# Two decode-attention blocks on one core: the last projection in two PSUM banks with two copiers, and both output stores on SyncE's queue

## Chip, cores, metric

One Trainium2 chip, one core of it. The metric is the device time of one execution in microseconds (us). The kernel before takes 2563.64 us (median of six runs, 2563.62 to 2563.99).

## The reference

Two independent blocks, A and B, each a single-token decode step: 8 batch rows, 32 heads of width 128, a cache of 4096 keys and values per head, all in bf16. Their outputs are concatenated.

```python
def block(x, k_cache, v_cache, wq, wo):            # once for A, once for B
    q = (x @ wq).reshape(B, 1, H, 128).transpose(0, 2, 1, 3)
    scores = einsum("bhqd,bhkd->bhqk", q, k_cache) * 128 ** -0.5
    o = einsum("bhqk,bhkd->bhqd", softmax(scores), v_cache)
    return o.transpose(0, 2, 1, 3).reshape(B, 1, H * 128) @ wo     # wo: 4096 x 1024
```

## The kernel before

The kernel streams all caches once through a ring of three 8 MB SBUF slots. Each engine is given a list of operations, and a dependency becomes a semaphore wait only where it is needed. Only the end matters here. Block B's output weights `wo` arrive in four pieces of 20, 8, 3 and 1 of 32 rows, so that little is left to multiply when the last piece lands. Block A is c = 0, block B is c = 1 = NC - 1.

```python
NT, DT = 4, 256                       # 4 column tiles of 256 output columns
wo_cuts = ((0, 20), (20, H - 4), (H - 4, H - 1), (H - 1, H))
proj, pv_ps = ps("proj"), ps("pv")    # two PSUM banks; pv_ps is free after the last attention tile
...
def make_proj(c):
    w = tile_of("wo", c)
    for i, (r0, r1) in enumerate(wo_cuts if c == NC - 1 else ((0, H),)):
        def emit(e, r0=r0, r1=r1):
            for r in range(r0, r1):
                for q in range(NT):
                    col = r * D + q * DT
                    x = e.matmul(proj[32 * q:32 * (q + 1), 0:DT], on_sb[:, c, r:r + H * B:HQ],
                                 w[:, col:col + DT], start=(r == 0), stop=(r == H - 1), tile_position=(0, 32 * q))
            return x
        opProj[c] = add("pe", emit, [opNorm[c], opT[("wo", c, i)], c_pad, opEv.get(c - 1)])
    opEv[c] = add("dve", lambda e: e.tensor_copy(orow[:, c, :], proj[:, 0:DT]), [opProj[c]])
    outs.append(dma(out[...], orow[0:128:32 // B, c, :], ("out", 0),
                    [opEv[c]] if c == NC - 1 else [opEv[c], opT[("wo", NC - 1, len(wo_cuts) - 1)]],
                    "sp" if c == NC - 1 else "act"))
...
make_norm(1); make_proj(0); make_proj(1)
```

The four matmuls of a row go to four column tiles of the array and run side by side. The trace shows that one `matmul` is two PE instructions, a weight load and a matmul. The first store (A's half of the output) waits for the last weight piece, presumably so that it does not get between the loads.

## Time and profile before

| | before |
|---|---|
| time, median of 6 runs | 2563.64 us |
| span of the profiled execution | 2562.6 us |
| DMA | over 90% busy in all 40 slices, 432 GB/s |
| VectorE, the busiest engine | 85% |

The lines below are from the page of the kernel before: DMA activity by slice, the queues that carry instructions and data, and the chain of waits.

```profile
DMA  9999999999999999999999999999999999999999
...
q1 hardware_dynamic: 19476, 1107.32, 99.9%
q8 instruction: 7, 0.11, 0.0%
...
DMA 52%; DVE 28%; issue 16%; PE 4%; ACT 0%; another core or an unknown queue 0%; DVEq 0%; SPq 0%
```

The kernel is bound by its loads. The change touches only what comes after the last attention tile, so its effect can only be in the last microseconds. They are in the timeline (start in us, duration in us, engine, line, operation, what it writes and reads, how many; in brackets PE's idle time before and what ended it):

```profile
2552.50 4.24 PE L431 MATMUL proj<-ring,on_sb 128*32 128x256 bf16 x80 [5.70 <-DMA ring<-in_B_wo_dram]
2557.31 0.86 PEld L431 LDWEIGHTS proj<-ring,on_sb 128*32 128x32 bf16 x32 [0.82 <-DMA ring<-in_B_wo_dram]
2557.31 1.10 PE L431 MATMUL proj<-ring,on_sb 128*32 128x256 bf16 x32 [0.58 <-DMA ring<-in_B_wo_dram]
...
2559.17 0.96 PE L431 MATMUL proj<-ring,on_sb 128*32 128x256 bf16 x16 [0.76 <-DMA ring<-in_B_wo_dram]
...
2559.84 0.65 ACTq L208 DMA_DIRECT2D out_dram<-orow  x1
2560.19 0.42 DVE L435 CAST orow<-proj 128x256 bf16<-128x256 f32 x1 [12.91 <-PE proj L431]
2560.64 0.69 SPq L208 DMA_DIRECT2D out_dram<-orow  x1
```

Every piece's matmuls wait for a DMA: PE is always ahead of the weights. After the last weights come four matmuls, one copy of 0.42 us and the store.

### The profile page before, as it was taken

What the parts mean: (1) busy time and instruction counts of PE and PEld (TensorE: products, weight loads), DVE (VectorE), ACT (ScalarE), POOL (GpSimd) and SP (SyncE); (2) the same over time, 40 slices, a digit from 0 to 9 for tenths busy, and PEclk for the clock granted to TensorE, in tenths of its full rate; (3) what the DMA queues carried; (4) which work ended last, traced back from release to release, by engine and by line L of the source; (5) the groups of instructions that cost most, each with busy time, mean ns of one, the idle gap of its engine ahead of it and who ended that gap; (6) DMA issues with size and microseconds to landing.
All of it is one profiled execution on the core that took longest, in us unless ns stands there. A gap on an engine that the chain in (4) does not pass through costs nothing.

```text
span 2562.6 us, 18832 instructions
## 1 busy us (share of the span) xinstructions
PE 1118.0 (44%) x7712; PEld 397.3 (16%) x7712; DVE 2170.6 (85%) x1042; ACT 129.8 (5%) x401; POOL 2.6 (0%) x15
## 2 busy tenths in 40 slices
PE   2443443443444444444434444444444434434435
PEld 0111111111111111111111111111111111111112
DVE  3898898898898898898898888988988988988983
ACT  1100000000000000000000000000000000000000
POOL 0000000000000000000000000000000000000000
PEclk8767676766767766766767666766757666666657
DMA  9999999999999999999999999999999999999999
GB/s 425 427 438 430 436 432 436 432 436 432 436 432 436 430 437 430 436 432 435 432 435 431 435 433 433 435 433 435 432 436 432 435 433 435 433 435 433 435 433 394
DMA packets 19554, 1107.51 MB, mean 432 GB/s; under 512 B 2184, under 2 KB 2248, under 8 KB 2520
## 3 DMA queue, kind: packets, MB, share of 16 engines
q1 hardware_dynamic: 19476, 1107.32, 99.9%
q8 instruction: 7, 0.11, 0.0%
q10 hardware_dynamic: 68, 0.05, 0.0%
q14 instruction: 3, 0.02, 0.0%
HBM read 1107.33 MB, written 0.03 MB: 432 GB/s over the span
## 4 chain that ended last, share of the span: by engine, by line
DMA 52%; DVE 28%; issue 16%; PE 4%; ACT 0%; another core or an unknown queue 0%; DVEq 0%; SPq 0%
DMA ring<-in_A_k_cache_dram 25%; DMA ring<-in_B_k_cache_dram 25%; DVE ring L330 10%; DVE ring L335 10%; PE red L345 4%; DVE s_sb L353 4%; DVE PM L370 3%; DMA ring<-in_B_wo_dram 2%; DVE rmax L359 1%; DVE rtmp L360 0%; ACT PM L291 0%; PE o L285 0%; DVEq L135 0%; DVE ngm L363 0%
## 5 line engine op out<-in xcount | busy, mean ns | idle before, releaser
L330 DVE TENSOR_TENSOR ring<-ring,qbc 128x8192 bf16<-128x8192 bf16 x256 | 1131.8, 4421 | 309.7 <-DMA ring<-in_B_k_cache_dram 152.9
L345 PE MATMUL red<-ring,ident 128*128 128x512 bf16 x2048 | 782.6, 552 | 1391.7 <-DVE ring L335 1391.7
L335 DVE TENSOR_TENSOR ring<-ring 128x4096 bf16<-128x4096 bf16 x256 | 582.2, 2274 | 0.0
L345 PEld LDWEIGHTS red<-ring,ident 128*128 128x128 bf16 x2048 | 239.1, 127 | 1843.5 <-DVE ring L335 1494.1
L353 DVE TENSOR_REDUCE s_sb<-red 128x64 f32<-128x1024 f32 x256 | 311.9, 1218 | 3.5 <-PE red L345 3.5
L382 PE MATMUL pv<-ring,PM 128*32 128x512 bf16 x4096 | 273.3, 414 | 4.7 <-DVE PM L370 4.7
L370 DVE TENSOR_TENSOR PM<-pe,own_h 128x2048 bf16<-128x2048 bf16 x64 | 146.2, 2285 | 0.7 <-ACT pe L365 0.7
L382 PEld LDWEIGHTS pv<-ring,PM 128*32 128x32 bf16 x4096 | 103.6, 103 | 187.4 <-issue 114.3
L319 ACT ACTIVATE qbc<-misc 128x128 bf16<-128x128 f32 x64 | 17.7, 277 | 1091.7 <-PE misc L317 1091.7
L365 ACT ACTIVATE pe<-s_sb,ngm 128x256 bf16<-128x256 f32 x64 | 32.5, 508 | 466.7 <-DVE ngm L363 466.7
L390 ACT ACTIVATE accS<-pv 128x512 bf16<-128x512 f32 x64 | 38.2, 597 | 352.9 <-PE pv L382 352.9
L399 PEld LDWEIGHTS o<-accS,E 128*32 128x32 bf16 x1024 | 31.3, 100 | 49.6 <-issue 48.4
L399 PE MATMUL o<-accS,E 128*32 128x32 bf16 x1024 | 38.1, 185 | 0.7 <-ACT accS L390 0.7
L405 ACT ACTIVATE o_sb<-o 32x32 f32 (+1 forms) x64 | 11.8, 185 | 452.4 <-PE o L399 444.5
L359 DVE TENSOR_REDUCE rmax<-s_sb 128x1 f32<-128x256 f32 x64 | 26.9, 420 | 2.2
L435 DVE CAST orow<-proj 128x256 bf16<-128x256 f32 x2 | 0.8, 424 | 27.4 <-PE proj L431 27.4
L431 PE MATMUL proj<-ring,on_sb 128*32 128x256 bf16 x256 | 12.7, 377 | 15.8 <-DMA ring<-in_A_wo_dram 8.7
L305 DVE COPY qT<-misc 128x64 bf16<-128x64 bf16 x8 | 3.5, 435 | 18.6 <-PE misc L301 18.6
L312 ACT ACTIVATE qst<-qT 128x128 bf16 (+1 forms) x64 | 18.7, 293 | 1.9 <-DVE qT L305 1.9
L360 DVE TENSOR_SCALAR rtmp<-half,rmax 128x32 f32<-128x32 f32 x64 | 15.4, 241 | 2.3
L363 DVE TRANSPOSE_TENSOR_REDUCE ngm<-rtmp 128x1 f32<-128x32 f32 x64 | 13.6, 212 | 2.2
L317 PE MATMUL misc<-ident,qst 128*128 128x128 bf16 x64 | 14.7, 230 | 0.9 <-ACT qst L312 0.9
(33 smaller groups left out, 66.1 us busy)
## 6 DMA issues: line engine op xcount, KB each, us to landing
ring<-in_B_wo_dram SPq DMA_DIRECT2D x1, 5120.0 KB, 33.2
ring<-in_B_wo_dram SPq DMA_DIRECT2D x1, 2048.0 KB, 37.8
ring<-in_B_wo_dram SPq DMA_DIRECT2D x1, 768.0 KB, 39.1
ring<-in_A_k_cache_dram SPq DMA_DIRECT2D x32, 39.9
ring<-in_A_v_cache_dram SPq DMA_DIRECT2D x32, 27.8
ring<-in_B_k_cache_dram SPq DMA_DIRECT2D x32, 39.8
ring<-in_B_v_cache_dram SPq DMA_DIRECT2D x32, 27.8
ring<-in_B_wo_dram SPq DMA_DIRECT2D x1, 256.0 KB, 39.3
```

The costliest lines, as they stand in the source:

```text
L312: return e.activation(qst[:, n % 2, :].rearrange("p (j m) -> p j m", m=MP), from_.unsqueeze(2).to_broadcast([128, HQ, MP]), ACTF.Copy)
L319: opQbc[n] = add("act", lambda e: e.activation(qbc[:, n % 2, :], misc[:, 0:Dh], ACTF.Copy), [opQb[n], _at(opMul, NR * (n - 2) + NR - 1)])
L330: opMul[s] = add("dve", lambda e: e.tensor_tensor(v, v, qbc[:, n % 2, :].unsqueeze(1).to_broadcast([128, CT, Dh]), ALU.mult), [opT[("k", n ...
L335: return add("dve", lambda e: e.tensor_tensor(v[:, :, 0:64], v[:, :, 0:64], v[:, :, 64:128], ALU.add), [opMul[s]])
L345: i = e.matmul(dst, ident[:], v[:, g, :, j, :], start=(j == 0), stop=(j == 3))
L353: opRed[s] = add("dve", lambda e: e.tensor_reduce(s_sb[:, n % 2, r * CT:(r + 1) * CT], red_ps[s % 2][:, :].rearrange("p (t w) -> p t w", w ...
L359: m = add("dve", lambda e: e.tensor_reduce(rmax[:], s_sb[:, n % 2, :], AX.X, ALU.max), [opRed[NR * n + NR - 1]])
L365: opExp[n] = add("act", lambda e, at: e.activation(pe[:], s_sb[:, n % 2, :], ACTF.Exp, bias=ngm[:, n % 2:n % 2 + 1], scale=scale, accum_ou ...
L370: opPM[n] = add("dve", lambda e: e.tensor_tensor(PM[:], pe[:].unsqueeze(2).to_broadcast([128, T, HQ]), own_h[:].unsqueeze(1).to_broadcast( ...
L382: i = e.matmul(pv_ps[32 * q:32 * (q + 1), :], PM[:, t:t + 4, :].rearrange("p t j -> p (t j)"), v[:, t * Dh:(t + 4) * Dh], start=(g == 0), ...
L390: opAcc[n] = add("act", lambda e: e.activation(accS[:], pv_ps[:], ACTF.Copy), [opPV[n], _at(opExt, n - 1)])
L399: x = e.matmul(to, E[:, i, PH - 1 - u:PH - 1 - u + MB], accS[:, i * 128 + H * u:i * 128 + H * (u + 1)], start=(i == 0 and u == 0), stop=(i ...
```

## The change

Intent: the single copy of 256 columns is the only arithmetic left between the last matmul and the store. With the columns in two banks, VectorE and ScalarE can each copy half at the same time; the Trainium skill, "TensorEngine Tiling (Array Packing)", section "PSUM Bottleneck", gives the same advice, to use both engines to empty PSUM (what that was worth here is measured in e8). The first store also leaves ScalarE, whose queue is then free for its copy.

```diff
+            banks = (proj, pv_ps) if c == NC - 1 else (proj,)
+            dt = DT // len(banks)
             for i, (r0, r1) in enumerate(wo_cuts if c == NC - 1 else ((0, H),)):
-                ... 4 matmuls of DT = 256 columns a row into proj ...
+                for f, bank in enumerate(banks):
+                    def emit(e, r0=r0, r1=r1, f=f, bank=bank):
+                        for r in range(r0, r1):
+                            for q in range(NT):
+                                col = r * D + q * DT + f * dt
+                                x = e.matmul(bank[32 * q:32 * (q + 1), 0:dt], on_sb[:, c, r:r + H * B:HQ],
+                                             w[:, col:col + dt], start=(r == 0), stop=(r == H - 1), tile_position=(0, 32 * q))
+                        return x
+                    opProj[(c, f)] = add("pe", emit, [..., opAcc[NQ - 1]] + opEv.get(c - 1, []))
-            opEv[c] = add("dve", lambda e: e.tensor_copy(orow[:, c, :], proj[:, 0:DT]), [opProj[c]])
+            opEv[c] = [add("dve", lambda e: e.tensor_copy(orow[:, c, 0:dt], proj[:, 0:dt]), [opProj[(c, 0)]])]
+            if len(banks) == 2:
+                opEv[c].append(add("act", lambda e: e.activation(orow[:, c, dt:DT], pv_ps[:, 0:dt], ACTF.Copy), [opProj[(c, 1)]]))
-    first store: waits for the last piece (len(wo_cuts) - 1), on "act"
+    first store: waits for the last piece but one (len(wo_cuts) - 2), on "sp"
```

More of the change, by code (lines that the diff above doesn't have):

```diff
@@ L424, in make_proj @@
             w = tile_of("wo", c)
+            banks = (proj, pv_ps) if c == NC - 1 else (proj,)
+            dt = DT // len(banks)
             for i, (r0, r1) in enumerate(wo_cuts if c == NC - 1 else ((0, H),)):
-                def emit(e, r0=r0, r1=r1):
-                    for r in range(r0, r1):
-                        for q in range(NT):
-                            col = r * D + q * DT
-                            x = e.matmul(proj[32 * q:32 * (q + 1), 0:DT], on_sb[:, c, r:r + H * B:HQ],
-                                         w[:, col:col + DT], start=(r == 0), stop=(r == H - 1), tile_position=(0, 32 * q))
-                    return x
-                opProj[c] = add("pe", emit, [opNorm[c], opT[("wo", c, i)], c_pad, opEv.get(c - 1)])
-            opEv[c] = add("dve", lambda e: e.tensor_copy(orow[:, c, :], proj[:, 0:DT]), [opProj[c]])
+                for f, bank in enumerate(banks):
[6 more added lines that the diff above has]
+                        return x
+                    opProj[(c, f)] = add("pe", emit, [opNorm[c], opT[("wo", c, i)], c_pad, opAcc[NQ - 1]] + opEv.get(c - 1, []))
+            opEv[c] = [add("dve", lambda e: e.tensor_copy(orow[:, c, 0:dt], proj[:, 0:dt]), [opProj[(c, 0)]])]
+            if len(banks) == 2:
+                opEv[c].append(add("act", lambda e: e.activation(orow[:, c, dt:DT], pv_ps[:, 0:dt], ACTF.Copy), [opProj[(c, 1)]]))
             outs.append(dma(out[:, 0, c * D:(c + 1) * D].rearrange("b (q n) -> q b n", q=NT), orow[0:128:32 // B, c, :],
-                            ("out", 0), [opEv[c]] if c == NC - 1 else [opEv[c], opT[("wo", NC - 1, len(wo_cuts) - 1)]],
-                            "sp" if c == NC - 1 else "act"))
+                            ("out", 0), opEv[c] if c == NC - 1 else opEv[c] + [opT[("wo", NC - 1, len(wo_cuts) - 2)]], "sp"))
         x_sb = ring[0:B, 2, 0:NC * D].rearrange("p (c d) -> p c d", c=NC)
```

## The prediction

> What bounds the kernel now. The page shows DMA busy above 90% in all 40 slices at a mean of 432 GB/s, while VectorE, the busiest engine, is at 85%; the chain of waits gives 52% to DMA. Everything before the last projection is untouched by the change. Only the tail can move. In the timeline its last steps are: the last weight piece (1 of 32 rows, 256 KB) ends its landing at about 2559.75 us; PE's last four matmuls run from 2559.80 to 2560.13; VectorE copies 128x256 from 2560.19 to 2560.61 (424 ns); SyncE issues the second store at 2560.64; the span ends at 2562.56. So 2.8 us come after the last load. The last 1.9 us are the store from issue to completion; the Trainium skill, "DMA: Bandwidth & Descriptors", section "Anatomy of one DMA", gives about 2.0 us as a DMA's fixed cost, and this trace agrees with 1.9. The change does not touch that part.
>
> What the change does. (1) The last tile's 128 matmuls of 256 columns become 256 of 128 columns, with as many weight loads again. Streamed columns stay the same. Four column tiles run together: in the first piece a group of four 256-column matmuls takes 213 ns at the half clock, later 109 ns at the full clock, so columns and not issue set the pace; L399's 32-column pairs of load and matmul take only 25 ns on one column tile. I estimate 107 and 55 ns for four of 128 columns, so PE's time is unchanged (4.2, 1.1, 0.6 and 0.33 us in the four pieces), and PE still waits for each piece. The first bank's last matmul ends about 53 ns earlier than now (estimate), the second's when it ends now. (2) The one copy of 424 ns becomes two in parallel: VectorE 128x128 about 310 ns (estimate, between 207 ns for 8 columns and 424 ns for 256), ScalarE 277 ns (the same shape at L319 takes 277). The pair ends about 2560.46 instead of 2560.61. (3) The first store goes from ScalarE's queue to SyncE's, and waits for the third piece, not the fourth: issued near 2559.15, it takes 0.65 us of SyncE, which is free by 2559.8, before the second store is ready. It leaves ScalarE (now issuing for 0.65 us from 2559.84) free for its copy.
>
> On the critical path: about 0.15 us saved, 0.006% of the time.
>
> What could cost it back. The longer PE program is 256 instructions or 16 KB more, and the page's instruction queue q8 shows fetches of 16 KB each (7, 0.11 MB); the Trainium skill, "Runtime: NRT & Kernel Launch", section "Instruction fetch mechanics", says refills come in 16 KiB blocks. They take about 1.03 us of one DMA engine each, and an eighth is due near 2557.9. On a DMA engine still loading the last piece it would delay that landing by up to 1 us; I give that one chance in five.
>
> Predicted 2563.5 us, 8 in 10 between 2562.7 and 2564.6. Faster by over 2%: 0.003; within 2%: 0.994; slower: 0.003.
>
> What would show it: the second store's issue 0.1 to 0.2 us nearer the last weight landing; a ScalarE copy near 280 ns beside a VectorE copy near 310 ns; matmul time of the four pieces unchanged; eight q8 packets. What would make it wrong: a weight-load limit at 128 columns pushing the first piece's 160 matmuls past 6 us, so that PE runs behind the landings (up to 1 us later); the instruction fetch; the first store delaying the second in the same queue.

## The result

| | before | after |
|---|---|---|
| median of 6 runs | 2563.64 us | 2563.95 us |
| range | 2563.62 to 2563.99 | 2563.57 to 2564.97 |
| ratio | | 1.0002, 95% interval 0.9989 to 1.0015 |

A ratio is the mean time of one kernel's fast runs over that of the other's of the same rounds, so not quite the ratio of the medians. The time is inside the predicted range, but the 0.15 us that the prediction counted are not there: the median is 0.3 us higher, and the runs spread over 1.4 us instead of 0.4. With that spread the 0.3 us is not clear of noise; what can be followed is where the time goes in the profiled execution.

From the page after:

```profile
DMA  9999999999999999999999999999999999999999
...
q1 hardware_dynamic: 19512, 1107.34, 99.9%
q8 instruction: 8, 0.13, 0.0%
...
DMA 51%; DVE 28%; issue 16%; PE 4%; another core or an unknown queue 0%; ACT 0%; DVEq 0%; SPq 0%
```

One instruction fetch more, as predicted; the rest is the same. The timeline after, from the second piece on (SyncE's line merges its two store issues, at 2559.24 and 2561.05), and then one line of the critical chain:

```profile
2557.34 0.39 PEld L434 LDWEIGHTS proj<-ring,on_sb 128*32 128x32 bf16 x13 [0.58 <-DMA ring<-in_B_wo_dram]
2557.34 0.55 PE L434 MATMUL proj<-ring,on_sb 128*32 128x128 bf16 x12 [0.32 <-DMA ring<-in_B_wo_dram]
2559.14 0.53 PE L434 MATMUL proj<-ring,on_sb 128*32 128x128 bf16 x19 [1.25 <-issue]
...
2559.24 2.36 SPq L208 DMA_DIRECT2D out_dram<-orow  x2
...
2560.42 0.25 PE L434 MATMUL pv<-ring,on_sb 128*32 128x128 bf16 x3
2560.64 0.29 DVE L438 CAST orow<-proj 128x128 bf16<-128x128 f32 x1 [14.33 <-PE proj L434]
2560.70 0.28 ACT L440 ACTIVATE orow<-pv 128x128 bf16<-128x128 f32 x1 [30.27 <-PE pv L434]
```

```profile
2557.89 1.25 issue
```

Here is the surprise. PE starts the second piece's 64 matmuls at 2557.34 and stops after 13 weight loads and 12 matmuls, for 1.25 us, with "issue" as the releaser: the profile shows no semaphore and no DMA that it waited for. When it resumes at 2559.14, the third piece's semaphore is filled within 0.01 us (2559.15), so PE has lost its lead: 84 matmuls are still to do, and the last piece's semaphore, at 2559.78, releases only the final 8 of them. The last matmul ends at 2560.67 instead of 2560.14.

The copies themselves did what was planned: 0.29 and 0.28 us side by side instead of 0.42.

The table follows the end of each profiled execution. The weights' landing is the end of the last packet of the load, its closing one of 4 bytes (the semaphore by which PE sees the landing is full only 0.4 to 0.5 us later, at 2559.75 in before); the other columns are instruction times. All are read from the traces.

| kernel | last weights | last matmul ends | copies end | last store issued | span ends | weights to end | store to end |
|---|---|---|---|---|---|---|---|
| before | 2559.33 | 2560.14 | 2560.61 | 2560.64 | 2562.55 | 3.23 | 1.91 |
| after | 2559.30 | 2560.67 | 2560.98 | 2561.05 | 2562.86 | 3.57 | 1.81 |

The landing itself differs between executions (2558.96 to 2559.44 over all kernels here), so "weights to end" is the number to compare.

### What the gap could be

The trace's packet records give the time of each 16 KB packet on the instruction queue q8, and the weight loads of the last projection can be counted. Put together for the profile of after:

```
weight load 44 of the last projection starts     2553.58
q8 packet of 16384 bytes                         2556.59, took 1.09
PE stops between load 172 and its matmul         2557.57
PE resumes                                       2559.14
next q8 packet of 16384 bytes                    2560.25
```

A packet of 16 KB holds 256 instructions (the Trainium skill, "Runtime: NRT & Kernel Launch", section "Instruction fetch mechanics"), or 128 pairs of load and matmul, and 172 is 44 + 128. My theory: PE's program is fetched in pages of 256 instructions, and a page is asked for when PE enters the one before it (e5 will show that PE's reading of instructions counts here, which can be a few ahead of the matmuls). The doubled projection is 512 instructions long, so that it always holds two page boundaries, and PE goes through a page in about 3.4 us (128 pairs at 27 ns). The page that begins at matmul 172 was asked for at about 2553.6. On the DMA engines, full of weights, its packet began only 3.0 us later, and PE could use it 1.5 us after the packet's end. The kernel before has one boundary in the last projection, near matmul 44, whose page was asked for in block A's projection (packet at 2545.53). It too has a packet at 2556.48, but by the same count that one is for instructions behind its last matmul.

Rivals: the switch between two PSUM banks, or the second copier, stops PE; matmuls of 128 columns are limited by weight loads; the gap was a chance of one profile.

### The profile page after: what moved, and what is told of

Read it like the earlier page. It is cut to its first block, busy times and chain, and to the rows that moved or that the text cites. A ratio compares the mean times of both kernels' runs of the same rounds, so it can differ in the third digit from the quotient of the medians.

```text
span 2562.9 us, 19090 instructions
## 1 busy us (share of the span) xinstructions
PE 1116.2 (44%) x7840; PEld 398.1 (16%) x7840; DVE 2170.4 (85%) x1042; ACT 130.0 (5%) x402; POOL 2.6 (0%) x15
## 4 chain that ended last, share of the span: by engine, by line
DMA 51%; DVE 28%; issue 16%; PE 4%; another core or an unknown queue 0%; ACT 0%; DVEq 0%; SPq 0%
DMA ring<-in_A_k_cache_dram 25%; DMA ring<-in_B_k_cache_dram 25%; DVE ring L330 10%; DVE ring L335 10%; PE red L345 4%; DVE s_sb L353 4%; DVE PM L370 3%; DMA ring<-in_B_wo_dram 2%; DVE rmax L359 1%; DVE rtmp L360 0%; ACT PM L291 0%; DVEq L135 0%; DVE ngm L363 0%; PE o L285 0%
## 5 line engine op out<-in xcount | busy, mean ns | idle before, releaser
L434 PE MATMUL proj<-ring,on_sb 128*32 128x256 bf16 (+1 forms) x256 | 9.6, 321 | 18.3 <-DMA ring<-in_A_wo_dram 10.0
```

## The experiments

Ten runs, each of five rounds against before on the same chip, all with correct results. All intervals hold 1.0. The runs of before lie between 2563.39 and 2563.82 on all three chips that these experiments used.

### e1_double_one_bank: the doubling alone

```diff
-            banks = (proj, pv_ps) if c == NC - 1 else (proj,)
+            banks = (proj, proj) if c == NC - 1 else (proj,)
-    e.matmul(bank[32 * q:32 * (q + 1), 0:dt], ..., start=(r == 0), ...)
+    e.matmul(bank[32 * q:32 * (q + 1), f * dt:(f + 1) * dt], ..., start=(r == 0 and f == 0), ...)
+    one copy of 256 columns on VectorE, stores as before
```

> Edit: the last tile's matmuls are doubled (256 of 128 columns) but all into the one old bank, one VectorE copy of 256 columns, stores as before. Theory (instruction page): the extra 256 PE instructions put a page boundary inside the second weight piece; PE stalls there for 1 to 1.5 us with no semaphore to wait for, its last matmul ends near 2560.6 instead of 2560.1, the copy stays 424 ns; whole time 0.4 to 0.6 us above before. Rival (two banks or two copiers cost it): no stall in the second piece, time within 0.1 us of before. Rival (128-column matmuls are too slow for the weight-load path): the first piece's 160 matmuls take over 5 us and no gap stands inside a piece.

Measured: 2564.86 us (2563.93 to 2565.41) against 2563.62 (2563.53 to 2563.80). PE's timeline:

```profile
2552.67 3.78 PE L434 MATMUL proj<-ring,on_sb 128*32 128x128 bf16 x160 [6.27 <-DMA ring<-in_B_wo_dram]
2557.48 0.41 PE L434 MATMUL proj<-ring,on_sb 128*32 128x128 bf16 x12 [1.02 <-DMA ring<-in_B_wo_dram]
2559.28 2.47 PE L434 MATMUL proj<-ring,on_sb 128*32 128x128 bf16 x84 [1.39 <-issue]
```

The same gap at the same place, after 12 matmuls of the second piece, with one bank and one copier, and with the old stores. So the doubled instructions bring it, not the banks. The first piece's 160 matmuls take 3.8 us, so that rate is not the limit either. I expected 0.4 to 0.6 us of loss and measured 1.2. After the gap the 84 matmuls took 2.47 us, against 1.53 in the profile of after. The windows view of both kernels says why (columns: window, its length, PE busy with the number of matmuls, granted clock, DMA share, GB/s). First after, then e1:

```profile
2559.00:2561.00 2.00, 1.53 (x84) 1.00 0.08 19
```

```profile
2559.00:2561.00 2.00, 1.72 (x66) 0.50 0.04 13
```

In e1 the granted clock was 0.5 after the gap. The Trainium skill, "TensorE: Matmul & The Clock Gate", Part 1, says that idle windows of about 3.4 us, which run freely, put the clock to half; this trace agrees in the two levels 0.5 and 1.0, and all stretches of one clock in before, after and e1, but the last that the profile cuts off, are multiples of 3.41 us. An idle window need not be empty, though: in the 3.4 us before e1's clock fell (2555.35 to 2558.76) PE was busy for 1.5. How long PE then takes for the rest depends on the clock it gets.

### e2_pad40 and e3_pad108: the boundary moved

```diff
+        def emit_pad(e):
+            for _ in range(40):                    # e3: 108
+                x = e.matmul(pv_ps[0:32, 256:264], ident[:, 0:32], ident[:, 0:8], start=True, stop=True, tile_position=(0, 0))
+            return x
+        add("pe", emit_pad, [opAcc[NQ - 1]])
         make_proj(0)
```

The tiny matmuls run while PE waits for block A's weights anyway, and their results are thrown away. They only move the rest of the program against the pages.

> Edit: the changed kernel with 40 tiny matmuls (80 PE instructions) in PE's idle time before the projections, so that the page boundaries fall 40 matmuls earlier, at about matmul 4 and 132 of the last tile instead of 44 and 172. Theory: the stall moves into the first piece (near matmul 132) and ends by about 2558.3; PE catches up before the last piece lands, its last matmul ends near 2560.1, the copies by 2560.5, the time 0.1 to 0.2 us under before and 0.4 to 0.6 under the changed kernel. Rival (the stall belongs to the bank switch or to the second piece): it stays after 12 matmuls of the second piece and the time is that of the changed kernel.

> Edit: the same with 108 tiny matmuls, boundaries at about matmul 64 and 108 earlier: 108 is 172 minus 64, so they fall at about 64 and 108+... counted modulo 128 at matmul 64 before wrap, that is at 64 and 192 of the last tile or, if the count is modulo 128 from 172, at 64 and 192. Theory: the page of matmul 192 is asked for later than in the changed kernel (when matmul 64 is issued, about 0.5 us later), PE stalls at matmul 192 inside the second piece until about 2559.7, and the time is 0.2 to 0.6 us above the changed kernel's. Rival (no page effect): the time is the changed kernel's within 0.15 us.

The text for e3 is muddled in its counting; what it settles on is 64 and 192 (44 and 172 less 108, plus 128 each). Measured: e2 2564.95 us (2564.40 to 2565.14), e3 2563.91 us (2563.32 to 2564.40), before 2563.62. PE's timeline of e2:

```profile
2552.34 2.36 PE L434 MATMUL proj<-ring,on_sb 128*32 128x128 bf16 x80 [6.64 <-DMA ring<-in_B_wo_dram]
2554.45 1.63 PE L434 MATMUL pv<-ring,on_sb 128*32 128x128 bf16 x52
2558.48 0.97 PE L434 MATMUL pv<-ring,on_sb 128*32 128x128 bf16 x28 [2.40 <-issue]
```

and of e3:

```profile
2552.13 2.36 PE L434 MATMUL proj<-ring,on_sb 128*32 128x128 bf16 x80 [7.01 <-DMA ring<-in_B_wo_dram]
2554.25 2.38 PE L434 MATMUL pv<-ring,on_sb 128*32 128x128 bf16 x80
2556.93 0.72 PE L434 MATMUL proj<-ring,on_sb 128*32 128x128 bf16 x32 [0.30 <-DMA ring<-in_B_wo_dram]
2559.02 0.71 PE L434 MATMUL pv<-ring,on_sb 128*32 128x128 bf16 x31 [1.37 <-issue]
```

The gap moved to matmul 132 (80 + 52) with 40 pairs of padding and to matmul 192 (160 + 32) with 108, just where the page arithmetic puts it. In e2 it is inside a piece that had wholly landed. None of the three rivals explains that.

The times missed. I expected e2 to hide the gap and to gain; it lost 1.3 us. Its page was asked for at the start of the first piece (2552.3), the packet began 3.6 us later, and PE stood from 2556.1 to 2558.5; the clock stayed at 0.5, and the 124 remaining matmuls took until 2561.66. e3 had the full clock and ended 0.2 us later, from the weights' landing, than before (3.46 against 3.23): less than after in its profile (3.57), not more as I expected, since only 64 matmuls were left behind its gap. In the times, e3's mean is 0.31 us above before, which is what the rival text expected (the changed kernel's 0.27 to 0.42); it is the place of the gap that speaks for the pages here, not the time.

### e4_early_piece: the page asked for earlier

```diff
-        wo_cuts = ((0, 20), (20, H - 4), (H - 4, H - 1), (H - 1, H))
+        wo_cuts = ((0, 10), (10, 20), (20, H - 4), (H - 4, H - 1), (H - 1, H))
```

> Edit: the changed kernel with the first weight piece of 20 rows cut into two of 10, so PE starts the last tile some 3 to 6 us earlier and asks for the next instruction page earlier. Theory: no stall in any piece, last matmul near 2560.1, copies end near 2560.45, time 0.1 to 0.2 us under before. Rival (rate of the matmuls or the bank switch): PE still ends near 2560.6 and the time stays at the changed kernel's.

Measured: 2563.68 us (2563.40 to 2563.70) against 2563.62. PE enters the last projection at 2547.2 instead of 2552.5; the q8 packet is at 2551.06, and from then on PE has no gap inside a piece:

```profile
2557.30 1.08 PE L434 MATMUL proj<-ring,on_sb 128*32 128x128 bf16 x32 [2.80 <-DMA ring<-in_B_wo_dram]
2558.16 1.07 PE L434 MATMUL pv<-ring,on_sb 128*32 128x128 bf16 x32
2559.17 0.54 PE L434 MATMUL proj<-ring,on_sb 128*32 128x128 bf16 x12
...
2559.93 0.32 PE L434 MATMUL pv<-ring,on_sb 128*32 128x128 bf16 x4
```

The same 256 matmuls, the same two banks, and no gap. The mean is 0.03 us under before on its chip, where the changed kernel's is 0.27 us above (e10, below; standard error of this difference about 0.2), and the spread is 0.3 us instead of 1.2 to 1.4. But the expected gain over before was not there.

### e5_before_early: is an early start worth something by itself?

The same edit of the cuts, in the kernel before.

> Edit: control for the early piece: the kernel before (128 matmuls of 256 columns, one copy, old stores) with the first weight piece of 20 rows cut into two of 10. Theory: the kernel before has one page boundary in the last tile (near matmul 44), whose page was asked for long before, so it has no stall to lose; its time stays within 0.1 us of before (0.2 us above where PE happens to run at the half clock in the last pieces). Rival (an earlier start of the last tile is worth time by itself): it gains 0.2 us or more.

Measured: 2563.89 us (2563.73 to 2563.96) against 2563.69 (2563.52 to 2563.82): 0.2 us slower, not faster. PE runs the last pieces at half clock, where before's had 1.0:

```profile
2557.00:2559.00 2.00, 1.64 (x32) 0.50 0.64 255
```

Its last matmul ends 0.96 us after the weights, against 0.81. So e4's cure costs something of its own, in both kernels: the work is spread out, and the clock stays at 0.5 up to the last matmul in all four profiles with the early piece and nothing to fill PE's waits (e4, e5, e7, e8).

e5 also corrects the theory in one point. Its packet for what follows the page of matmul 44 began at 2550.95, 1.6 us before load 44 started (2552.51), while PE stood in front of matmul 40 for its weights. So the request does not wait for the first load of the page to run: PE reads some pairs ahead. e2 shows the same in block A's projection, where its boundary lies at matmul 4: the packet came at 2535.28, and PE waited there for A's weights until 2540.1.

### e6_stores_only: the stores alone

In the kernel before, only the two stores are as in the change.

> Edit: the kernel before with the change's stores alone (both on SyncE's queue, the first waiting for the third piece). Theory: the first store is issued near 2559.2 and is out of the way; the second is issued at the same time after the copy as before, its issue perhaps 0.15 us shorter (538 ns in the changed kernel against 688 before), so the time is 0 to 0.15 us under before. Rival (the two stores in one queue delay the second): 0.1 us or more above before.

Measured: 2563.62 us (2563.37 to 2563.67) against 2563.69; means 2563.55 and 2563.65. From the issue of the last store to the span's end took 1.81 us, against 1.91. The traces agree without exception: in the eight profiles where SyncE has issued the first store too, it is 1.79 to 1.81 us, and in the four where ScalarE has issued it 1.91 or 1.92. SyncE's issue of the second store is 537 to 541 ns in the first group and 688 to 699 ns in the second. Whether the shorter issue comes from a recent issue on the same engine or from the shared queue stays open.

### e7_early_act_store and e8_early_dve_both: the parts of the copy

Both start from e4. In e7 the first store is back on ScalarE behind the last piece; in e8 VectorE makes both copies.

> Edit: e4_early_piece with the first store put back on ScalarE's queue, waiting for the last piece. Theory: ScalarE's issue of about 0.65 us starts with the last landing (about 2559.85) and its copy can only start after it, near 2560.5 instead of 2560.3, ending near 2560.8; time 0.2 to 0.35 us above e4. Rival (the place of the first store is without effect): within 0.1 us of e4.

> Edit: e4_early_piece with both copies of the last tile on VectorE. Theory: two copies of 293 ns one after the other, ending near 2560.8 (or 2560.75 at the full clock) against 2560.58 for the pair; time about 0.15 to 0.25 us above e4, so splitting the copy without the second engine is worse than the single 424 ns copy. Rival (the copy is not on the critical path): within 0.05 us of e4.

Measured: e7 2564.16 us (2563.93 to 2564.22), e8 2563.80 us (2563.54 to 2563.86), before 2563.69 on their chip. Mean against before on its own chip: e4 -0.03, e7 +0.46, e8 +0.07. ScalarE in e7:

```profile
2559.92 0.65 ACTq L208 DMA_DIRECT2D out_dram<-orow  x1
2560.62 0.28 ACT L440 ACTIVATE orow<-pv 128x128 bf16<-128x128 f32 x1 [28.07 <-DVE orow L438]
```

The copy stands behind the store's issue, which ends at 2560.57 (VectorE's copy, which the profile names, ended at the same time, but the program has no wait of one for the other), and ends at 2560.90 instead of 2560.58, and the second store also loses e6's 0.1 us; I had not counted that, so the loss against e4 is 0.49 us in the means instead of 0.2 to 0.35. So moving the first store is not an extra: without it the second copier would be no gain. VectorE in e8:

```profile
2560.24 0.29 DVE L438 CAST orow<-proj 128x128 bf16<-128x128 f32 x1 [14.04 <-PE proj L434]
2560.45 0.28 DVE L440 CAST orow<-pv 128x128 bf16<-128x128 f32 x1
```

Its two copies start 0.21 us apart although each lasts 0.29, and end at 2560.73. The loss against e4 is 0.10 us in the means, less than the expected 0.15 to 0.25 and not clear of the spread; from the weights to the end e8's profile is no longer than e4's (3.17 against 3.19). From the last matmul to the end of the copies it is 0.48 us in before, 0.43 in e8 and 0.33 in e4: splitting the copy saved a little even without the second engine, against what I expected, and the second engine saved another 0.10. Nearly half of that is taken back by a cost of the pair: with two copiers SyncE waits for two semaphores, which the trace shows as one more instruction (17 ns) in front of the store's issue, and 72 ns pass from the last copy's end to the issue in e4 and 73 in after, against 27 ns in before and 28 in e8.

### e9_early_warm: no stall and a warm PE

```diff
+                def emit_warm(e, n=(10, 8, 2, 0, 0)[i]):
+                    for _ in range(n):
+                        x = e.matmul(red_ps[0][:, 0:512], ident[:], accS[:], start=True, stop=True)
+                    return x
+                if c == NC - 1 and i < 3:
+                    add("pe", emit_warm, [opRed[NS - 1], opAcc[NQ - 1]])
```

> Edit: e4_early_piece with 20 matmuls of 128x512 (results thrown away) in PE's waits between the weight pieces (10, 8, 2). Theory: e4 had no page stall but ran its last pieces at the half clock, which cost it about 0.1 to 0.15 us at the end; with PE kept busy the granted clock is 1.0 in the last two pieces, four matmuls of 128 columns start every 55 to 65 ns there instead of 107, the second bank ends near 2560.1 and ScalarE's copy near 2560.45, and the time is 0.1 to 0.25 us under e4 and under before: the gain of 0.15 us that the prediction counted. Rival (the half clock in e4 was without effect): the time is e4's, 2563.4 to 2563.7.

Measured: 2563.57 us (2563.36 to 2563.72) against 2563.66 (2563.39 to 2563.79). The windows of e4, then of e9:

```profile
2557.00:2559.00 2.00, 1.70 (x64) 0.50 0.66 257
2559.00:2561.00 2.00, 1.25 (x44) 0.50 0.04 12
```

```profile
2557.00:2559.00 2.00, 1.40 (x65) 1.00 0.61 243
2559.00:2561.00 2.00, 1.12 (x33) 1.00 0.04 12
```

The clock is 1.0, and four matmuls of 128 columns start every 60 to 65 ns. In this profile the time from the last weights to the span's end is 3.07 us, against 3.23 in before and 3.19 in e4: 0.15 us less than before. But this is not the predicted 0.15 us, which was all in the copies: against before, the copies gave 0.15 us and the second store 0.11 from its issue on, which the prediction did not count, while the last matmul came 0.05 us later after the weights and the second semaphore cost 0.05. In the times the mean is 0.09 us under before and 0.06 under e4 (each against before on its own chip), less than expected, with overlapping runs; the median, 2563.57, lies where the rival put it. So the clock is shown by the profile, and its worth in time is not.

### e10_after_again: the changed kernel once more

> The changed kernel once more, on the same chip as e9 and with five rounds. Theory: PE stalls again after 12 matmuls of the second piece, for 1.0 to 1.7 us; the run is slow (2564.5 or more) where the profile shows the half clock after the stall and 2563.5 to 2564.1 where it shows the full clock; the spread of its runs is over 0.5 us while before's is under 0.35 us. Rival (the stall was a chance of one profile): no gap inside a piece.

Measured: 2563.75 us (2563.45 to 2564.68); before 2563.66. PE's timeline:

```profile
2557.05 0.40 PE L434 MATMUL proj<-ring,on_sb 128*32 128x128 bf16 x12 [0.30 <-DMA ring<-in_B_wo_dram]
2558.49 0.53 PE L434 MATMUL proj<-ring,on_sb 128*32 128x128 bf16 x20 [1.04 <-issue]
```

The same gap after the same 12 matmuls, at the full clock: this profiled run was 2563.45 us, a little under the bound that I had given for it. Here the page came at 2558.49 and PE could catch up by 2560.01, 0.94 us after the weights (before: 0.81). So the gap is there in both profiles of the changed kernel, but what it costs depends on when the page comes and on the clock: by the time from the weights to the end this execution was even shorter than before's (3.14 against 3.23). The spread of the five runs is 1.2 us, before's nine 0.4 (I had said under 0.35). Only one execution of each is profiled, so that the slow runs had the half clock is supported by e1 and e2, not shown run by run.

### The ends together

| kernel | last weights | last matmul ends | copies end | last store issued | weights to end | store to end |
|---|---|---|---|---|---|---|
| e1 doubling alone | 2559.44 | 2561.75 | 2562.22 | 2562.24 | 4.73 | 1.92 |
| e2 boundary at 132 | 2559.09 | 2561.66 | 2561.99 | 2562.06 | 4.77 | 1.80 |
| e3 boundary at 192 | 2558.96 | 2560.22 | 2560.54 | 2560.61 | 3.46 | 1.81 |
| e4 early piece | 2559.25 | 2560.25 | 2560.58 | 2560.65 | 3.19 | 1.79 |
| e5 before, early piece | 2559.33 | 2560.29 | 2560.77 | 2560.80 | 3.39 | 1.92 |
| e6 stores only | 2559.19 | 2560.04 | 2560.52 | 2560.55 | 3.17 | 1.81 |
| e7 first store on ScalarE | 2559.40 | 2560.34 | 2560.90 | 2560.99 | 3.52 | 1.92 |
| e8 VectorE copies both | 2559.38 | 2560.30 | 2560.73 | 2560.76 | 3.17 | 1.80 |
| e9 early piece, warm PE | 2559.41 | 2560.27 | 2560.60 | 2560.68 | 3.07 | 1.81 |
| e10 after again | 2559.07 | 2560.01 | 2560.33 | 2560.40 | 3.14 | 1.81 |

## Why the prediction was right or wrong

The predicted time and "within 2%" were right, for the reason given: 2559 of 2563 us are a stream of loads that the change does not touch. This hit says little about the tail: the range was 1.9 us wide, and the kernel before lies in it as well.

The 0.15 us of gain did not come. The failed step is "PE's time is unchanged (4.2, 1.1, 0.6 and 0.33 us in the four pieces), and PE still waits for each piece". It counted columns and not instructions. The columns' rate was nearly right: the first piece took 4.5 us in after's windows, and four matmuls of 128 columns start every 107 ns at the half clock in e4 and every 60 to 65 ns at the full clock in e9, where 55 had been estimated. But PE stood for 1.25 us for its own next instruction page (e1 and the two pads show that cause, e4 its cure), and its last matmul ended 0.53 us later than in before's profile (in e10's, from the weights' landing, only 0.13 us later).

The prediction named the instruction fetch as the risk, and the eighth q8 packet came, at 2560.25, when the weights had landed; the packet that PE waited for was the seventh. The mechanism it gave was wrong: it let the packet delay the last weights on a DMA engine. The last weights landed as before (2559.30 and 2559.33); it was PE, the reader of the page, that waited. It also put the packet at 2557.9; there was one at 2556.59 and one at 2560.25.

The copies were right: 292 and 277 ns for 310 and 277. One small term was missing: the pair makes SyncE wait for two semaphores, 73 ns from copy to store instead of 27.

The stores were right that the first does not get in the way, and e7 shows that ScalarE needed to be freed. The step "The change does not touch that part", of the 1.9 us from store to completion, was wrong by 0.1 us in the change's favour (1.81 against 1.91, e6).

So the sum of the change, in its own profile: 0.53 us lost at the last matmul, about 0.16 won from there to the end of the copies (0.31 against 0.47), 0.05 lost at the second semaphore, 0.11 won after the issue: 0.31 us lost, and the spans differ by 0.31. With the stall away and the clock full (e9) the time from weights to end is 0.15 us under before. That this is the 0.15 predicted is partly luck: two losses of 0.05 us that the prediction did not count are made up by the store's 0.11, which it did not count either.

No version is clearly better than both kernels. e6 and e9 are 0.1 us under before in their means, with overlapping runs. e6 is the simpler one.

## What to carry to other kernels

Splitting a matmul in two leaves the streamed columns equal but doubles PE's instructions, and a short burst that holds two instruction pages can run out of program while the DMA queues are full; an "issue" gap in the middle of a group of equal matmuls that moves with unrelated padding is the sign of it. Count the page boundaries in the burst before saving tenths of a microsecond behind it: the kernel before, with one boundary, had no gap, and starting the burst earlier took the gap away (e4). When only a tail is changed, compare from the last load's landing, since the landing itself varied by 0.5 us between these executions.

## What the Trainium skill lacked or had wrong

- "Runtime: NRT & Kernel Launch", section "Instruction fetch mechanics": it says that the next 16 KiB block is fetched while the current one runs, and that crossing a boundary is "mostly hidden". The block size agrees. Not hidden here: PE stood 1.0 to 2.4 us in five profiles (after, e1, e2, e3, e10). It lacks the latency under load: in these five profiles the packet began 2.8 to 3.6 us after the first load of the page before it while the weights were streaming (1.9 to 4.0 us in the profiles without a gap; in e5 before that load), and the next one 1.1 to 1.5 us after PE resumed behind the gap, when the weights were nearly done; it took about 1.1 us itself, and PE resumed 1.2 to 1.5 us after its end.
- "TensorE: Matmul & The Clock Gate", section "Back-to-back issue gap": for 128 columns it gives about 81 ns per matmul in a stream of load and matmul pairs, and N/2.4 + 2.5 ns for a matmul alone, and in that section nothing for column tiles. Here four such pairs on four column tiles together started every 60 to 65 ns at the full clock (e9), and every 107 ns at the half clock (e4), which agrees with its N/1.2 for one.
- "DMA: Bandwidth & Descriptors", section "Anatomy of one DMA — SWDGE (gpsimd) path": its fixed cost of about 2.0 us is for the path that GpSimd issues; I found none for a store that SyncE issues. From the last store's issue to the end it was 1.79 to 1.81 us when SyncE had issued another store 1.3 to 3.0 us before, and 1.91 or 1.92 when its last issue was 40 us back.
- No page that I read has the cost of waiting for a second semaphore before a DMA issue: 73 ns instead of 27 ns from the last copy's end to the issue (after against before).
